# The third block's moved pairs: all tiles' scores in one half slice, a third buffer for transposed blocks, values around the second block's last second layer

## The chip, the cores and the metric

One Trainium2 chip, one of its cores. The time is device microseconds of one execution of the whole program; the kernel before took 667.09 us (median of three runs, 666.11 to 667.18).

## What is computed

Banded attention with a few global columns, then a two-layer network on its output, in float32. Batch 4, 8 heads, 768 positions, head size 64, so the network sees 3072 tokens of width 512 and has a hidden width of 2048.

```
scores = scale * q @ k^T                  # per batch and head, 768 x 768
keep   = (col < n_global) | (0 <= row - col < n_local)        # 8 and 96
scores = where(keep, scores - slope[head] * dist, -1e9)
a      = exp(scores - max) / (sum + 1e-9)
x      = (a @ v) as 3072 x 512
h      = x @ w_in                         # 512 x 2048
g      = h * clip(h + 3, 0, 6) / 6
out    = g @ w_out                        # 2048 x 512
```

## The kernel before

**Blocks, pairs, slices.** The 3072 tokens are cut into eight blocks of 384 (three tiles of 128). A block's attention is done by pairs of heads, four pairs to a block, numbered through: pairs 8 to 11 belong to the third block. Its network is done in 16 slices of the hidden width (f0 to f15). Every float32 product is done as three matmuls of a high and a low part (`w1h`, `w1l`, `xh`, `xl`, `gh`, `gl`).

**A slice** has two halves. First half: `first` (L161), 12 matmuls into a bank `hp`; then `gate` (ScalarE L178, VectorE L179) and the high part `gh` (GpSimd L185); the low part `gl` (VectorE L192) follows. Second half: `finish`, which runs `second` (L195), 9 matmuls, for the slice **before** it. So TensorE's order is first f9, second f8, first f10, second f9 and so on, and the `gh` and `gl` of a slice have the time of a second half and a first half to get ready. `halves` (L448) is a generator that stops after each half; between two stops the caller runs a list of closures, a *unit*, which holds attention work of a later block.

**A pair** in these units has these steps:

- `split(0..2)` (L810): ScalarE writes `q1` and GpSimd the high part of `kx` (step 0), VectorE writes `q2` (step 1, L828) and the low part of `kx` (step 2, L831), and step 2 then issues the load of the keys and queries of the pair two ahead. The buffers hold one pair, so step 0 has to come after the last score matmul of the pair before.
- `scores(t)` (L836) for t = 0, 1, 2: four matmuls into a bank, VectorE adds the distances and takes the least (L865), ScalarE the exponentials (L869).
- `sum_up`, `normalize(t)`: reciprocals on VectorE, then six GpSimd multiplications (L889).
- `spread(t)` (L904): VectorE turns 32 x 32 squares (L914) into a buffer `blocks`, and SyncE's queue writes it to DRAM (`there`); the first tile of pairs 8 to 11 has one transpose, the others two.
- `fetch` (L919): four transfers bring it back as `weights` with the squares in place.
- `values` (L932): twenty or twenty-four matmuls with `v` (L941), then ScalarE and VectorE write `xh`, `xl` of the block (`put_x`, L150), then the `v` of the pair two ahead is loaded.

**The stage of the change** ("one") runs from the last first-block slice to the start of the third block's network. In it the second block's slices f8 to f15 run, 16 half slices, and beside them the attention of pairs 9 to 11 (pair 8 was done earlier) and the splits of pair 12. The second block's sums occupy the banks `sp`, `tp` and `xp`, so scores and values share the three banks `acc`, in rotation. `rest_of_third` (L631) builds the units; `banded` (L589 to L600) makes the pools and runs them.

**What sets the order.** `in_order` (L621) ties TensorE, SyncE and GpSimd to the order in which the code is written. The order on VectorE and ScalarE is chosen by the scheduler when the program is built. All transfers of this stage are issued by SyncE, one after the other, and one that waits holds up those behind it.

After this stage the network of blocks three to eight runs in the same way, with the attention of the next block in the units of `attention` (L661), which the change doesn't touch except by the number of `blocks` buffers.

Of the kernel before, what the change touches and what calls it, by code (L numbers as in the profile page):

```python
# [20 lines left out]
NT = 3  # L21
# [4 lines left out]
NF = DF // P  # L26
# [16 lines left out]
EARLY = 9  # L43
# [7 lines left out]
ORDER = "101001010010010100100"  # L51
# [8 lines left out]
class Kernel:  # L60
# [433 lines left out]
    def banded(self, flag):  # L494
# [12 lines left out]
        with ExitStack() as early, ExitStack() as words:  # L507
            x0 = self.x_tiles(self.pool("x0", 1, ctx=early, side="right"))
            xs = [x0, self.x_tiles(), self.x_tiles()]
# [8 lines left out]
            with ExitStack() as ctx:  # L518
# [7 lines left out]
                pairs = [Pair(self, n, xs[n // NPAIR], True) for n in range(EARLY)]  # L526
# [55 lines left out]
            next_f, todo = [FIRST, 0], []  # L582
# [4 lines left out]
                pass  # L587
            self.decoded_to(2 * NF - 1)
        self.attending(self.ctx, 2, 3, 2, side="right")  # L589
        self.bp = self.pool("bp", 2, side="right")  # L590
        self.there = self.pool("there", 2, bass.MemoryType.DRAM)
        self.op = self.pool("op", 3, side="right")
        self.stage = "one"
        units, ahead = self.rest_of_third(xs[2])
        for k, _ in enumerate(self.halves([(1, f, xs[1], acc1) for f in range(next_f[1], NF)], True)):
            for unit in units[k]:
                unit()
        self.finish()
        for unit in units[k + 1]:
            unit()  # L600
        self.stage = "layers"
        x = xs[2]
        for i in range(2, len(self.blocks)):
            units, x_next = [], None
            if i + 1 < len(self.blocks):
                x_next = self.x_tiles()
                units, ahead = self.attention(i + 1, x_next, ahead)
            else:
                units = [[]] * 4 + [[lambda: self.doubt(flag)]]
# [7 lines left out]
            x = x_next  # L617
# [10 lines left out]
                        mybir.DependencyClass.NoSync, mybir.DependencyReason.DATA), reason="in_order")  # L628
                last[i.engine] = i.name

    def rest_of_third(self, x):  # L631

        units = [[] for _ in range(2 * NF)]
        pairs = [Pair(self, n, x, False) for n in range(EARLY, 3 * NPAIR + 1)]
        for k in range(3):
            pairs[0].split(k, False)
        units[1] += [lambda: self.load_next(EARLY, False)]
        for p, (me, after) in enumerate(zip(pairs, pairs[1:])):
            at = units[4 * p + 1:]
            for t, k in enumerate((0, 0, 1)):  # L640
                at[k].append(lambda t=t, me=me: me.scores(t)())
            last = after is pairs[-1]
            if not last:
                at[1].append(lambda after=after: after.split(0))
            k = 1 if last else 2
            at[k] += [me.sum_up] + [lambda t=t, me=me: me.normalize(t) for t in range(NT)]
            if not last:
                at[2].append(lambda after=after: after.split(1))
            at[k + 1] += [lambda t=t, me=me: me.spread(t) for t in range(NT)]
            if not last:  # L650
                at[3].append(lambda after=after: after.split(2))
            at[k + 1] += [me.fetch]
            if last:
                for k in range(3):
                    at[3 + k].append(lambda k=k, after=after: after.split(k))
                units[2 * (NF - ORDER.count("1"))] += [lambda a=pairs[p - 1]: a.values("x"), lambda me=me: me.values("s")]
        if EARLY % 2:
            units[9].append(lambda: pairs[0].values("x"))
        return units, pairs[-1]

    def attention(self, i, x, first):  # L661

# [358 lines left out]
```

## Time and profile before

| | |
|---|---|
| time, median of three runs | 667.09 us |
| the profiled execution's own time | 666.31 us |
| its span (first to last instruction) | 664.5 us |
| TensorE idle by its list of waits, in stage "one" | 2.8 us on transfers, 1.1 us on GpSimd |
| TensorE idle by its list of waits, 207 us to the end | none listed |
| granted TensorE clock | 0.999 |

A line of the timeline has the start in us from the span's start, the duration, the engine, the code line, the operation, what it writes and reads, and how many instructions the line stands for; a bracket at its end gives the idle time of the engine before it and what ended that. PE is TensorE, DVE VectorE, ACT ScalarE, POOL GpSimd, SPq the transfers that SyncE issues. Matmuls are pipelined, so their durations overlap; time lost on TensorE is read from one start to the next.

### The profile page before, as it was taken

What the parts mean: (1) busy time and instruction counts of PE and PEld (TensorE: products, weight loads), DVE (VectorE), ACT (ScalarE), POOL (GpSimd) and SP (SyncE); (2) the same over time, 40 slices, a digit from 0 to 9 for tenths busy, and PEclk for the clock granted to TensorE, in tenths of its full rate; (3) what the DMA queues carried; (4) which work ended last, traced back from release to release, by engine and by line L of the source; (5) the groups of instructions that cost most, each with busy time, mean ns of one, the idle gap of its engine ahead of it and who ended that gap; (6) DMA issues with size and microseconds to landing.
All of it is one profiled execution on the core that took longest, in us unless ns stands there. A gap on an engine that the chain in (4) does not pass through costs nothing.

```text
span 664.5 us, 11420 instructions
## 1 busy us (share of the span) xinstructions
PE 649.1 (98%) x3933; PEld 581.2 (87%) x3933; DVE 430.1 (65%) x1147; ACT 288.5 (43%) x752; POOL 202.8 (31%) x377
## 2 busy tenths in 40 slices
PE   9989999999998999999999999999999999999997
PEld 7768899988878999899999989999998999989995
DVE  6888999997855776376653877457662776432222
ACT  6896877775433333244314333143331444121111
POOL 5662000002531543043340544225340444302110
PEclk9999999999999999999999999999999999999999
DMA  8676444432574566525663366524654255510001
GB/s 295 172 234 207 143 146 156 149 105 88 142 189 144 136 157 184 159 87 144 164 169 103 96 173 183 158 72 130 159 154 129 79 152 142 143 49 1 1 1 53
DMA packets 67316, 88.86 MB, mean 134 GB/s; under 512 B 10288, under 2 KB 52016, under 8 KB 67248
## 3 DMA queue, kind: packets, MB, share of 16 engines
q1 hardware_dynamic: 66960, 87.77, 46.2%
q8 instruction: 33, 0.54, 0.3%
q14 instruction: 35, 0.29, 0.1%
q10 hardware_dynamic: 288, 0.26, 0.1%
HBM read 65.08 MB, written 22.94 MB: 132 GB/s over the span
## 4 chain that ended last, share of the span: by engine, by line
PE 80%; DVE 10%; DMA 3%; ACT 2%; issue 2%; POOL 1%; SPq 0%; POOLq 0%; DVEq 0%; ACTq 0%
PE hp L167 35%; PE acc L199 33%; PE xp L941 3%; PE sp L854 2%; PE tp L941 2%; PE tp L854 2%; DMA there<-blocks 1%; DVE wz L422 1%; DVE wz L418 1%; DMA weights<-there 1%; ACT n L869 1%; DVE gl L192 1%; DVE g L179 1%; DVE wz L410 1%; POOL n L889 1%
## 5 line engine op out<-in xcount | busy, mean ns | idle before, releaser
L178 ACT ACTIVATE g<-hp,small 128x384 f32<-128x384 f32 x127 | 73.6, 579 | 248.4 <-PE hp L167 223.5
L167 PE MATMUL hp<-xh,w1h 128*128 128x384 f32 x512 | 174.2, 340 | 0.4 <-ACT w1h L426 0.4
L167 PE MATMUL hp<-xh,w1l 128*128 128x384 f32 x512 | 173.0, 338 | 0.5 <-DVE w1l L415 0.5
L167 PE MATMUL hp<-xl,w1h 128*128 128x384 f32 x512 | 172.1, 336 | 0.0
L185 POOL TENSOR_SCALAR gh<-g 128x384 fp32r<-128x384 f32 x104 | 56.2, 540 | 313.6 <-DVE g L179 287.1
L199 PE MATMUL acc<-w2h,gl 128*128 128x512 f32 x336 | 133.3, 397 | 0.2 <-DVE gl L192 0.2
L199 PE MATMUL acc<-w2l,gh 128*128 128x512 f32 x336 | 132.5, 394 | 0.0
L199 PE MATMUL acc<-w2h,gh 128*128 128x512 f32 x336 | 132.0, 393 | 0.0
L179 DVE SCALAR_TENSOR_TENSOR g<-g,hp 128x384 f32<-128x384 f32 x128 | 69.8, 545 | 69.6 <-ACT g L178 69.1
L869 ACT ACTIVATE n<-n,least 128x232 f32<-128x232 f32 (+1 forms) x192 | 89.1, 465 | 51.5 <-DVE least L865 50.1
L192 DVE TENSOR_TENSOR gl<-g,gh 128x384 fp32r<-128x384 f32 x128 | 79.7, 622 | 46.8 <-POOL gh L185 46.8
L889 POOL TENSOR_SCALAR n<-n,sums 128x232 f32<-128x232 f32 (+1 forms) x186 | 98.4, 545 | 35.7 <-DVE sums L880 24.4
L167 PEld LDWEIGHTS hp<-xh,w1h 128*128 128x128 f32 x512 | 96.4, 188 | 6.6 <-issue 1.9
L167 PEld LDWEIGHTS hp<-xl,w1h 128*128 128x128 f32 x512 | 96.2, 188 | 3.7
L167 PEld LDWEIGHTS hp<-xh,w1l 128*128 128x128 f32 x512 | 96.0, 188 | 1.0 <-DVE w1l L415 0.8
L199 PEld LDWEIGHTS acc<-w2h,gl 128*128 128x128 f32 x336 | 63.0, 188 | 15.3 <-DVE gl L192 2.0
L199 PEld LDWEIGHTS acc<-w2h,gh 128*128 128x128 f32 x336 | 63.3, 188 | 10.3 <-POOL gh L185 0.3
L199 PEld LDWEIGHTS acc<-w2l,gh 128*128 128x128 f32 x336 | 63.2, 188 | 10.3
L914 DVE STREAM_TRANSPOSE blocks<-n 128x256 f32<-128x256 f32 x127 | 49.4, 424 | 31.7 <-POOL n L889 19.4
L825 POOL TENSOR_SCALAR kx<-load 64x504 fp32r<-64x504 f32 (+1 forms) x46 | 36.2, 788 | 97.8 <-PE hp L167 96.0
L865 DVE CUSTOM_DVE_ANT_0 n<-sp,d 128x232 f32<-128x232 f32 (+1 forms) x70 | 23.7, 375 | 32.2 <-PE sp L854 31.7
L869 ACT ACTIVATION_READ_ACCUMULATOR n<-n,least 128x1 f32 x192 | 36.0, 188 | 0.0
(118 smaller groups left out, 745.3 us busy)
## 6 DMA issues: line engine op xcount, KB each, us to landing
wst<-w SPq DMA_DIRECT2D x32, 512.0 KB, 3.5
there<-blocks SPq DMA_DIRECT2D x58, 256.0 KB, 2.6
load<-pairs SPq DMA_DIRECT2D x23, 636.0 KB, 5.2
load<-pairs SPq DMA_DIRECT2D x32, 384.0 KB, 4.4
weights<-there SPq DMA_DIRECT2D x48, 192.0 KB, 3.7
weights<-there SPq DMA_DIRECT2D x44, 160.0 KB, 3.4
out<-o SPq DMA_DIRECT2D x23, 256.0 KB, 2.2
load<-pairs SPq DMA_DIRECT2D x8, 444.0 KB, 4.1
```

The source lines that it names most:

```text
L167: self.nc.tensor.matmul(hp, lhsT=self.w1(w, f)[:, kt, :], rhs=a[:, kt, :], start=(n == 0), stop=(n == 3 * NKT - 1))
L178: nc.scalar.activation(out=g, in_=hp, func=AF.Relu, bias=self.three, scale=1.0)
L179: nc.vector.scalar_tensor_tensor(out=g, in0=g, scalar=6.0, in1=hp, op0=ALU.min, op1=ALU.mult)
L185: self.nc.gpsimd.tensor_scalar(out=gh, in0=g, scalar1=1.0, scalar2=0.0, op0=ALU.mult, op1=ALU.add)
L192: self.nc.vector.tensor_tensor(out=gl, in0=g, in1=gh.bitcast(F32), op=ALU.subtract)
L199: self.nc.tensor.matmul(acc[tt], lhsT=a[:, tk], rhs=self.w2(w, f), start=(f == 0 and j == 0), stop=(f == NF - 1 and j == 2))
L825: nc.gpsimd.tensor_scalar(out=part["kx"][own, c], in0=k[own, c], scalar1=1.0, scalar2=0.0, op0=ALU.mult, op1=ALU.add)
L854: nc.tensor.matmul(sp[j][:, lo:W], lhsT=q[:, t], rhs=part["kx"][:, c], start=(m == 0), stop=(m == 1))
L869: nc.scalar.activation(out=e[:, j, lo:W], in_=e[:, j, lo:W], func=AF.Exp, bias=self.least[:, i:i + 1], scale=-1.0, accum_out=self.sums[:, ...
L889: nc.gpsimd.tensor_scalar(out=e[:, j, lo:W], in0=e[:, j, lo:W], scalar1=over, scalar2=0.0, op0=ALU.mult, op1=ALU.add)
L914: nc.vector.transpose(out=blocks[:, :, s].rearrange("p b j q -> p j b q"), in_=e[:, :, c:c + P].rearrange("p j (b q) -> p j b q", b=4))
L941: nc.tensor.matmul(xps[j * D:(j + 1) * D, t * P:(t + 1) * P], lhsT=vt[0:K, t, j * D:(j + 1) * D], rhs=self.part(t, j, c, K), start=(c == 0 ...
```

## The change

Per pair, the three score tiles move from two half slices (0, 0 and 1) into one, normalisation moves from the third half slice to the second and the transposes and the fetch from the fourth to the third; pair 11 had its normalisation and transposes there already. The splits of pairs 10 and 11 each move one half slice ahead. `blocks` gets three buffers in place of two, for the rest of the program. The values of pair 9 move from behind the second layer of f11 to behind the first layer of f13, one half slice on; those of pair 10 from behind the second layer of f15 to ahead of it; those of pair 11 stay behind it. The arithmetic is the same.

```diff
-        self.bp = self.pool("bp", 2, side="right")
+        self.bp = self.pool("bp", 3, side="right")
...
-        units, ahead = self.rest_of_third(xs[2])
+        units, pairs = self.rest_of_third(xs[2], NF - next_f[1])
         for k, _ in enumerate(self.halves([(1, f, xs[1], acc1) for f in range(next_f[1], NF)], True)):
             for unit in units[k]:
                 unit()
         self.finish()
-        for unit in units[k + 1]:
-            unit()
+        pairs[-2].values("s")
         self.stage = "layers"
-        x = xs[2]
+        x, ahead = xs[2], pairs[-1]
...
-    def rest_of_third(self, x):
+    def rest_of_third(self, x, slices):
...
         for p, (me, after) in enumerate(zip(pairs, pairs[1:])):
             at = units[4 * p + 1:]
-            for t, k in enumerate((0, 0, 1)):
-                at[k].append(lambda t=t, me=me: me.scores(t)())
             last = after is pairs[-1]
-            if not last:
-                at[1].append(lambda after=after: after.split(0))
-            k = 1 if last else 2
-            at[k] += [me.sum_up] + [lambda t=t, me=me: me.normalize(t) for t in range(NT)]
-            if not last:
-                at[2].append(lambda after=after: after.split(1))
-            at[k + 1] += [lambda t=t, me=me: me.spread(t) for t in range(NT)]
-            if not last:
-                at[3].append(lambda after=after: after.split(2))
-            at[k + 1] += [me.fetch]
-            if last:
-                for k in range(3):
-                    at[3 + k].append(lambda k=k, after=after: after.split(k))
-                units[2 * (NF - ORDER.count("1"))] += [lambda a=pairs[p - 1]: a.values("x"), lambda me=me: me.values("s")]
-        if EARLY % 2:
-            units[9].append(lambda: pairs[0].values("x"))
-        return units, pairs[-1]
+            at[0] += [lambda t=t, me=me: me.scores(t)() for t in range(NT)]
+            at[1] += [me.sum_up] + [lambda t=t, me=me: me.normalize(t) for t in range(NT)]
+            at[2] += [lambda t=t, me=me: me.spread(t) for t in range(NT)] + [me.fetch]
+            for k in range(3):
+                at[k + 3 if last else k].append(lambda k=k, after=after: after.split(k))
+        units[10].append(lambda: pairs[0].values("x"))
+        units[2 * slices - 1].append(lambda: pairs[-3].values("x"))
+        return units, pairs
```

The file gets twelve lines shorter, so line numbers behind the change are lower by twelve (L854 is then L842, L941 L929, L914 L902).

**TensorE at the end of the stage.** Before: the last matmul of the second layer of f14, the whole of that of f15 (it reads `gh_2427`), then the values of pair 10 (`weights_2240`) and pair 11 (`weights_2353`).

```order
L199 MATMUL xp_1029<-w2h1_1025,gl_2398 128x512
L199 MATMUL sp_1027<-w2h1_1025,gh_2427 128x512
L199 MATMUL sp_1027<-w2l1_1026,gh_2427 128x512
L199 MATMUL sp_1027<-w2h1_1025,gl_2432 128x512
L199 MATMUL tp_1028<-w2h1_1025,gh_2427 128x512
L199 MATMUL tp_1028<-w2l1_1026,gh_2427 128x512
L199 MATMUL tp_1028<-w2h1_1025,gl_2432 128x512
L199 MATMUL xp_1029<-w2h1_1025,gh_2427 128x512
L199 MATMUL xp_1029<-w2l1_1026,gh_2427 128x512
L199 MATMUL xp_1029<-w2h1_1025,gl_2432 128x512
L941 MATMUL acc_2461<-weights_2240,load1_73 64x128 x10
L941 MATMUL acc_2475<-weights_2353,load0_72 64x128 x10
```

Of the change, the same place (pair 10's weights are now `weights_2222`):

```order
L199 MATMUL xp_1029<-w2h1_1025,gl_2398 128x512
L929 MATMUL acc_2443<-weights_2222,load1_73 64x128 x10
L199 MATMUL sp_1027<-w2h1_1025,gh_2427 128x512
L199 MATMUL sp_1027<-w2l1_1026,gh_2427 128x512
L199 MATMUL sp_1027<-w2h1_1025,gl_2432 128x512
L199 MATMUL tp_1028<-w2h1_1025,gh_2427 128x512
L199 MATMUL tp_1028<-w2l1_1026,gh_2427 128x512
L199 MATMUL tp_1028<-w2h1_1025,gl_2432 128x512
L199 MATMUL xp_1029<-w2h1_1025,gh_2427 128x512
L199 MATMUL xp_1029<-w2l1_1026,gh_2427 128x512
L199 MATMUL xp_1029<-w2h1_1025,gl_2432 128x512
L929 MATMUL acc_2475<-weights_2353,load0_72 64x128 x10
```

Pair 10's values now stand between the last two second layers, and those nine matmuls between the values of pair 10 and of pair 11.

**ScalarE around pair 11's exponentials.** Before: the exponentials of its first tile (128 wide), the copy `xh` of pair 9, those of its second tile, a gate, the two `q1` of pair 12, those of its third tile, a gate.

```order
L869 ACTIVATE n_2273,sums_2271<-n_2273,least_80 128x128 x2
L153 CAST xh_151<-acc_2292 128x384
L869 ACTIVATE n_2283,sums_2271<-n_2283,least_80 128x232 x2
L178 ACTIVATE g_2319<-hp_2306,small_70 128x384
L824 ACTIVATE q1_2388<-load1_73 128x384
L824 ACTIVATE q1_2393<-load1_73 128x384
L869 ACTIVATE n_2325,sums_2271<-n_2325,least_80 128x232 x2
L178 ACTIVATE g_2383<-hp_2370,small_70 128x384
```

Of the change, the same stretch:

```order
L812 ACTIVATE q1_2388<-load1_73 128x384
L812 ACTIVATE q1_2393<-load1_73 128x384
L857 ACTIVATE n_2273,sums_2271<-n_2273,least_80 128x128 x2
L857 ACTIVATE n_2283,sums_2271<-n_2283,least_80 128x232 x2
L857 ACTIVATE n_2293,sums_2271<-n_2293,least_80 128x232 x2
L178 ACTIVATE g_2315<-hp_2302,small_70 128x384
L153 CAST xh_151<-acc_2328 128x384
L178 ACTIVATE g_2383<-hp_2370,small_70 128x384
```

The `q1` of pair 12, which read its load (`load1_73`), now stand ahead of all six exponentials of pair 11, and the gate of slice f13 behind them.

**SyncE's queue in the middle of the stage.** Before: pair 9's three writes to `there`, the load of pair 12 (`load1_73`, 1272 columns), pair 9's four fetches into `weights_2111`; then the same for pair 10 with the load of pair 13; then the `v` of pair 11 (768 columns).

```order
L916 DMA there_2112<-blocks_2113 512x1x64
L916 DMA there_2112<-blocks_2116 512x1x128
L916 DMA there_2112<-blocks_2120 512x1x128
L292 DMA load1_73<-pairs 128x1272
L923 DMA weights_2111<-there_2112 32x4x320 x4
L916 DMA there_2241<-blocks_2242 512x1x64
L916 DMA there_2241<-blocks_2245 512x1x128
L916 DMA there_2241<-blocks_2249 512x1x128
L292 DMA load0_72<-pairs 128x1272
L923 DMA weights_2240<-there_2241 32x4x320 x4
L292 DMA load0_72<-pairs 128x768
```

Of the change:

```order
L904 DMA there_2094<-blocks_2095 512x1x64
L904 DMA there_2094<-blocks_2098 512x1x128
L904 DMA there_2094<-blocks_2102 512x1x128
L911 DMA weights_2093<-there_2094 32x4x320 x4
L292 DMA load1_73<-pairs 128x1272
L904 DMA there_2223<-blocks_2224 512x1x64
L904 DMA there_2223<-blocks_2227 512x1x128
L904 DMA there_2223<-blocks_2231 512x1x128
L911 DMA weights_2222<-there_2223 32x4x320 x4
L292 DMA load0_72<-pairs 128x1272
L292 DMA load0_72<-pairs 128x768
```

Each fetch now stands ahead of the load that used to go before it, so the loads of pairs 12 and 13 are issued behind fetches that wait for the writes ahead of them.

## The prediction

> **What bounds the kernel now.** I read the page's head first, then the list of TensorE's waits, then the busy time by stage, then the timeline.
>
> ```profile
> span 664.5 us, 11420 instructions
> PE 649.1 (98%) x3933; PEld 581.2 (87%) x3933; DVE 430.1 (65%) x1147; ACT 288.5 (43%) x752; POOL 202.8 (31%) x377
> ```
>
> ```profile
> PE acc L941 <- DMA weights<-there: 2.8, 2, 1.7
> PE sp L199 <- POOL gh L185: 1.1, 1, 1.1
> ```
>
> ```profile
> 156.00:207.00 51.00, 47.16 (x293) 41.90 (x292) 33.10 (x96) 22.01 (x64) 16.83 (x33) 1.00 0.64 181
> 207.00:236.60 29.60, 29.60 (x162) 27.07 (x162) 22.89 (x64) 11.78 (x38) 12.93 (x23) 1.00 0.36 97
> 354.00:650.00 296.00, 296.00 (x1738) 268.63 (x1737) 161.23 (x421) 93.25 (x253) 93.44 (x166) 1.00 0.39 106
> ```
>
> TensorE sets the time. After 207 us it is busy without a gap (29.60 of 29.60 us, 296.00 of 296.00), so nothing is to be won there, only lost. In stage "one" 51.00 − 47.16 = 3.84 us are idle, and the two lines of the wait list that belong to it make 3.9 us. That stage is what the change rewrites. The timeline of TensorE there:
>
> ```profile
> 159.00 1.05 PE L854 MATMUL acc<-kx,q 128*128 128x128 f32 x8
> 159.88 0.34 PE L167 MATMUL hp<-xh,w1h 128*128 128x384 f32 x1
> ...
> 178.40 1.05 PE L854 MATMUL acc<-kx,q 128*128 128x128 f32 x8
> 180.52 1.32 PE L941 MATMUL acc<-weights,load 128*64 128x128 f32 x20 [1.07 <-DMA weights<-there]
> 181.77 0.44 PE L167 MATMUL hp<-xh,w1h 128*128 128x384 f32 x1
> ...
> 192.78 0.39 PE L199 MATMUL sp<-w2h,gh 128*128 128x512 f32 x1
> ...
> 194.63 0.40 PE L199 MATMUL xp<-w2h,gl 128*128 128x512 f32 x1
> 196.12 0.50 PE L199 MATMUL sp<-w2h,gh 128*128 128x512 f32 x1 [1.09 <-POOL gh L185]
> ...
> 198.52 1.32 PE L941 MATMUL acc<-weights,load 128*64 128x128 f32 x20
> 201.52 1.32 PE L941 MATMUL acc<-weights,load 128*64 128x128 f32 x20 [1.68 <-DMA weights<-there]
> 202.77 0.44 PE L167 MATMUL hp<-xh,w1h 128*128 128x384 f32 x1
> ...
> 204.96 0.60 PE L854 MATMUL sp<-kx,q 128*128 128x232 f32 x4
> 205.40 0.34 PE L167 MATMUL hp<-xh,w1h 128*128 128x384 f32 x1
> ```
>
> The reader should measure from start to start, since ends overlap. Eight score matmuls take 159.88 − 159.00 = 0.88, four take 205.40 − 204.96 = 0.44, one pair's values 181.77 − 180.52 = 1.25. What three waits cost:
>
> - Pair 9's values start at 180.52 where 178.40 + 0.88 = 179.28 was possible: **1.24**.
> - The second layer of f15 starts at 196.12. The step inside a second layer is (194.63 − 192.78) / 8 = 0.23, so 194.86 was possible: 1.26. It then takes 198.52 − 196.12 = 2.40 where nine steps are 2.08: 0.32 more. Together **1.58**.
> - Pair 11's values start at 201.52 where 198.52 + 1.25 = 199.77 was possible: **1.75**.
>
> In all **4.57 us**, an upper bound of what this change can win.
>
> **The change, part by part.** No matmul is added or removed; up to 178.40 TensorE does the same work in another order (the third score tile ahead of a first layer, not behind it).
>
> *Pair 9's values* go one half slice and a score tile later, and their fetch is issued earlier. They start behind the first layer of f13: 178.40 + 1.32 (three score tiles) + 2.1 = 181.8. In the profile before they could run at 180.52 with a fetch in the old place. The 1.24 go.
>
> *Pair 10's values* are ready long before (their chain starts ten us before pair 11's) and now stand ahead of the second layer of f15, so `gh` of f15 has 1.25 us more. That alone is a hair short of 1.26, but VectorE's side is eased too:
>
> ```profile
> 192.59 0.77 DVE L914 STREAM_TRANSPOSE blocks<-n 128x256 f32<-128x256 f32 x2 [0.67 <-DMA there<-blocks]
> 193.39 1.39 DVE L831 TENSOR_TENSOR kx<-load,kx 64x504 fp32r<-64x504 f32 x2
> 194.81 0.56 DVE L179 SCALAR_TENSOR_TENSOR g<-g,hp 128x384 f32<-128x384 f32 x1
> ```
>
> The gate of f15 stood behind pair 11's last transposes, which waited 0.67 for a `blocks` buffer. With a third one that wait is gone. The 1.58 go.
>
> *Pair 11's values* decide. When does TensorE come to them? The stretch from 181.77 to 194.86 (first f13 to second f14, without a wait) is 13.09 long with one score tile in it. Now: 178.40 + 1.32 + (13.09 − 0.44) + 1.25 (pair 9) = 193.6, + 1.25 (pair 10) + 2.08 (second f15) = **197.0**, where it was 201.52. When is `weights` there? Step by step, with rows of before:
>
> ```profile
> 162.72 0.93 ACT L824 ACTIVATE q<-load 128x384 fp32r<-128x384 f32 x2
> 163.55 0.48 ACT L869 ACTIVATE n<-n,least 128x232 f32<-128x232 f32 x1
> ...
> 180.83 0.40 ACT L869 ACTIVATE n<-n,least 128x128 f32<-128x128 f32 x1 [3.72 <-DVE least L865]
> ```
>
> ```profile
> 187.99 2.46 POOL L889 TENSOR_SCALAR n<-n,sums 128x128 f32<-128x128 f32 x6 [1.35 <-DVE sums L880]
> 190.42 0.51 POOL L185 TENSOR_SCALAR gh<-g 128x384 fp32r<-128x384 f32 x1
> ```
>
> Pair 11's scores end at 178.40 + 1.32 + 0.2 = 179.9. ScalarE then writes the two `q1` of pair 12 first (their buffer is free only now), 0.93, to 180.9; then six exponentials, 2 x 0.40 and 4 x 0.47, to 183.6; then the gate of f13, 0.5, to 184.1. VectorE's gate 0.55, to 184.7; GpSimd's `gh` of f13 0.51, to 185.2 (the sums are done meanwhile); six normalisations 2.46, to 187.7; the last two transposes 0.77, to **188.5**. Before, those ended at 192.59 + 0.77 = 193.36 and the values started at 201.52, 8.16 later: write, four fetches, landing. So 188.5 + 8.16 = **196.7**, 0.3 ahead of TensorE. That is no cover to speak of: a wait of 0 to 0.8 is what I put there, 0.3 as the value.
>
> *New costs.* (a) Pair 9's third score tile now writes the third `acc` bank at 159.88, which ScalarE is still emptying:
>
> ```profile
> 157.81 1.99 ACT L56 ACTIVATE o<-acc 128x512 f32<-128x512 f32 x3
> ```
>
> It ends at 159.80, so between nothing and 0.1. (b) VectorE, ScalarE and GpSimd get a pair's work in a lump, and the gates of f9 and f11 stand behind it on VectorE and ScalarE. For f11: pair 10's scores end near 170.2, `q1` 171.1, six exponentials 173.8, gate 174.3; VectorE does six reductions, two `q2` and two `kx`, which by these rows
>
> ```profile
> 163.73 1.33 DVE L828 SCALAR_TENSOR_TENSOR q<-load,q 128x384 fp32r<-128x384 f32 x2
> ...
> 164.98 0.87 DVE L192 TENSOR_TENSOR gl<-g,gh 128x384 fp32r<-128x384 f32 x1
> ...
> 166.30 0.57 DVE L831 TENSOR_TENSOR kx<-load,kx 64x400 fp32r<-64x400 f32 x1
> ```
>
> end at 174.0, the sums by 174.4, the gate at 174.9, `gh` at 175.5, `gl` at 176.1 to 176.4. The second layer of f11 wants `gh` at 176.31 and `gl` two matmuls later, 176.77. Cover 0.4 to 0.8 us: nothing lost, at worst 0.3. (c) Behind this stage the scheduler puts `gl` behind the third pair of transposes for pairs 12 to 15. The tightest place:
>
> ```profile
> 264.42 0.56 DVE L192 TENSOR_TENSOR gl<-g,gh 128x384 fp32r<-128x384 f32 x1 [0.33 <-POOL gh L185]
> ```
>
> ```profile
> 266.13 0.40 PE L199 MATMUL acc<-w2h,gl 128*128 128x512 f32 x1
> ```
>
> It is done at 264.98 and used at 266.13: 1.15 of cover against at most 0.77 more. Nothing lost.
>
> One rule of the Trainium skill speaks against (b): SBUF — State Buffer, section "Who interferes with whom", says that a VectorE instruction with two SBUF inputs and a GpSimd instruction that reads SBUF exclude each other for a whole instruction. The row of 0.87 above ran beside GpSimd's `kx`, where another `gl` has 0.56, so the trace shows a price of 0.3, not a full block. By the rule, GpSimd's two `kx` would be added whole to VectorE's lump, which would put `gh` of f11 about 1.6 later and cost about 0.8 us; the sum below would be −3.4 in place of −4.2.
>
> **Sum.** −4.57 + 0.3 (pair 11) + 0.1 (a and b) = **−4.2 us**. The profiled execution took 666.31 us (span 664.5 and 1.8 around it), which gives 662.1. The median of before is 0.8 above that execution and two of three runs lie at 667.1, so I put half the distance on it: **662.5**.
>
> **Rivals.** About 0.2%, 1.3 us, is what a measurement of this kernel can tell from no change.
>
> 1. *The wait stays at pair 11's values, over 1 us.* The two numbers that meet there, 197.0 and 196.7, are each sums of ten rows. And `q1` of pair 12 may be late: its load is issued behind pair 9's fetch. SyncE's queue before, and the landing times of the seven loads of this stage:
>
> ```profile
> 172.54 0.57 SPq L292 DMA_DIRECT2D load<-pairs  x1
> 174.68 1.76 SPq L923 DMA_DIRECT2D weights<-there  x4
> ```
>
> ```profile
> DMA to landing us min/median/max: 4.5/5.4/7.9
> ```
>
> Pair 9's last write goes out 2.5 earlier than before, so the fetch runs from 172.2 to 173.9 and the load lands at 173.9 + 5.4 = 179.3, or 181.8 with the longest landing; ScalarE wants it at 180.0. At worst 1.9 are added to pair 11's chain. Left of the gain: 2 to 3.5 us, 663.2 to 664.8. For it: the thin cover. Against: two ways of adding up give the same end.
>
> 2. *The lump becomes the bound* (no change): the second layers of f9, f11 and f13 each wait over 1 us for `gh`. It takes 2 to 3 us more in the lump than the rows give (the cover of `gh` is 0.8 at f11 and more at the others); three such stalls of 1.2 take 3.6 of the 4.2 back: 666.1. Against: every term in (b) is from the longer of the rows.
>
> 3. *Slower:* the same load as in rival 1, but so late that it holds ScalarE. Behind `q1` on that engine stand six exponentials and the gate of f13, and behind that GpSimd's normalisation and the second layer of f13. Each us that the load lands after 180.0 moves pair 11's values by one. It eats the whole gain from a landing at 184.2 and makes the kernel measurably slower from 185.5, which is 11.6 after its issue, where the longest of seven took 7.9. At a landing of 186 the time is 668.3.
>
> 4. *The change doesn't move what it says:* the order of before and after shows that the scores, values and fetches stand where the code puts them, so this is left only as rival 1, where the wait is renamed.
>
> **Chances.** Forecast (gain 3.5 to 4.6 us) 0.66; rival 1, 0.21; rival 2, 0.07; rival 3, 0.06. Faster by over 0.2% is the first two, 0.87; within 0.2% 0.07; slower 0.06. The range starts at 666.11 − 4.6, about 661.4, and reaches to the end of rival 1, 664.8; what is left out is rivals 2 and 3 and a little of both ends.
>
> **What would show it.** Right: the wait list names no `gh` and no `there` row in stage "one", or only pair 11's values with under 0.8; pair 9's values start behind the first layer of f13 at about 181.8; the block's network starts at about 198.3 where it was 202.77; the two `q1` of pair 12 start near 180.0; from there on every TensorE row is the old one moved by 4 to 4.5 us. Wrong: a bracket of over 1 us at pair 11's values (rival 1), brackets `<-POOL gh` at f9, f11 or f13 (rival 2), `q1` waiting on its load (rivals 1 and 3), or a gap on TensorE after the start of the third block's network, which would be the reordered transposes.

## The result, and the profile after

| | before | after |
|---|---|---|
| time, median (lowest to highest of six runs) | 667.13 us (666.11 to 668.55) | **662.27 us** (661.89 to 663.39) |
| the profiled execution's own time | 666.31 us | 662.71 us |
| its span | 664.5 us | 660.9 us |
| granted TensorE clock | 0.999 | 0.998 |
| stage "one" in the profile | 43.77 us | 39.66 us |

The ratio is 0.9928, with a 95% interval of 0.9915 to 0.9941: **faster by 0.7%**. "Stage" is here, and below, the stretch from the start of pair 9's first score matmul to the start of the third block's network (159.00 to 202.77 before).

The list of TensorE's waits after, whole:

```profile
PE xp L929 <- DVE xl L154: 2.4, 5, 1.1
PE xp L929 <- issue: 1.4, 1, 1.4
PE xp L362 <- DVE small L104: 0.9, 1, 0.9
PE hp L167 <- DVE w1l L415: 0.5, 1, 0.5
PE hp L167 <- ACT w1h L426: 0.4, 1, 0.4
PE tp L885 <- ACT pt L889: 0.3, 1, 0.3
PE acc L199 <- DVE gl L192: 0.2, 1, 0.2
```

The two rows that the prediction read before (2.8 us on `weights<-there`, 1.1 us on `gh`) are gone; what is left lies before 156 us, ahead of the stage. The busy time by stage, with the same three stretches moved by the time won:

```profile
156.00:203.50 47.50, 47.50 (x296) 42.49 (x295) 31.91 (x96) 21.59 (x64) 16.40 (x33) 1.00 0.67 196
203.50:233.10 29.60, 29.60 (x162) 27.02 (x161) 22.73 (x66) 11.77 (x36) 12.64 (x23) 1.00 0.39 104
350.00:646.00 296.00, 296.00 (x1738) 268.74 (x1737) 160.92 (x421) 93.34 (x253) 93.50 (x166) 1.00 0.39 107
```

TensorE is now busy for 47.50 of 47.50 us in the stage, and the two later stretches are as full as before. Its timeline:

```profile
159.32 1.56 PE L842 MATMUL acc<-kx,q 128*128 128x128 f32 x12
160.72 0.34 PE L167 MATMUL hp<-xh,w1h 128*128 128x384 f32 x1
...
176.71 0.39 PE L199 MATMUL sp<-w2h,gh 128*128 128x512 f32 x1
...
178.79 1.50 PE L842 MATMUL acc<-kx,q 128*128 128x128 f32 x12
180.13 0.34 PE L167 MATMUL hp<-xh,w1h 128*128 128x384 f32 x1
...
182.34 1.32 PE L929 MATMUL acc<-weights,load 128*64 128x128 f32 x20
183.59 0.50 PE L199 MATMUL sp<-w2h,gh 128*128 128x512 f32 x1
183.92 0.39 PE L199 MATMUL sp<-w2l,gh 128*128 128x512 f32 x1
184.15 0.40 PE L199 MATMUL sp<-w2h,gl 128*128 128x512 f32 x1
...
194.23 1.32 PE L929 MATMUL acc<-weights,load 128*64 128x128 f32 x20
...
197.73 1.32 PE L929 MATMUL acc<-weights,load 128*64 128x128 f32 x20
198.98 0.44 PE L167 MATMUL hp<-xh,w1h 128*128 128x384 f32 x1
```

The stage starts at 159.32, 0.32 later than before, so 0.32 is taken off a time of after to set it beside one of before. The three values blocks carry no bracket, and neither does any second layer. The stage takes 198.98 − 159.32 = 39.66, which is 4.11 less than before.

### The profile page after: what moved, and what is told of

It is laid out like the page before. It is cut to its first block, busy times and chain, and to the rows that moved or that the text cites. A ratio compares the mean times of both kernels' runs of the same rounds, so it can differ in the third digit from the quotient of the medians.

```text
span 660.9 us, 11414 instructions
## 1 busy us (share of the span) xinstructions
PE 649.6 (98%) x3933; PEld 581.9 (88%) x3933; DVE 427.6 (65%) x1147; ACT 288.1 (44%) x752; POOL 202.2 (31%) x377
## 4 chain that ended last, share of the span: by engine, by line
PE 86%; DVE 9%; ACT 2%; issue 2%; POOL 0%; POOLq 0%; DVEq 0%; ACTq 0%
PE hp L167 37%; PE acc L199 33%; PE xp L929 3%; PE sp L842 2%; PE tp L929 2%; PE tp L842 2%; PE sp L199 1%; ACT n L857 1%; DVE wz L422 1%; PE tp L199 1%; DVE wz L418 1%; PE xp L199 1%; DVE wz L410 1%; DVE g L179 1%; DVE gl L192 1%
## 5 line engine op out<-in xcount | busy, mean ns | idle before, releaser
L902 DVE STREAM_TRANSPOSE blocks<-n 128x256 f32<-128x256 f32 x127 | 48.8, 422 | 27.0 <-POOL n L877 26.8
```

The costliest lines, as they stand in the source:

```text
L902: nc.vector.transpose(out=blocks[:, :, s].rearrange("p b j q -> p j b q"), in_=e[:, :, c:c + P].rearrange("p j (b q) -> p j b q", b=4))
```

## The experiments

Twelve runs of eleven kernels were made, in three groups, each beside runs of the kernel before on the same chip. None leaves out a part of the computation. The stage's time is from one profiled execution, the median from all runs; "waits" are TensorE's in the stage.

| kernel | `blocks` | scores and normalisation | values 9 / 10 | median (lowest to highest, runs) | ratio, 95% interval | stage | waits of TensorE listed |
|---|---|---|---|---|---|---|---|
| before (two profiles) | 2 | old | old / old | 667.1, 666.1 and 667.1 in the three groups | | 43.77, 43.62 | 1.07, 1.09, 1.68; 1.02, 0.77, 1.86 |
| e1_buffer | 3 | old | old / old | 663.67 (663.08 to 664.83, 9) | 0.9946, 0.9931 to 0.9961 | 41.43 | 0.37, 1.10 |
| e2_ahead | 2 | old | old / new | 667.54 (665.82 to 669.38, 10) | 1.0005, 0.9987 to 1.0022 | 44.84 | 0.78, 3.03 |
| e3_lump | 2 | new | old / old | 668.58 (665.76 to 669.37, 10) | 1.0014, 0.9995 to 1.0033 | 44.95 | 2.61, 0.74 |
| e4_two | 2 | new | new / new | 667.21 (665.85 to 668.90, 10) | 1.0004, 0.9987 to 1.0022 | 44.37 | 0.34, 2.00, 0.37 |
| e7_both_old, e7_again | 3 | new | old / old | 663.11 (662.62 to 663.87, 4), 662.92 (662.31 to 665.09, 10) | 0.9951, 0.9934 to 0.9967; 0.9938, 0.9924 to 0.9952 | 41.20, 41.63 | 0.27, 0.82; 0.26, 1.30 |
| e9_moves_buffer | 3 | old | new / new | 663.84 (662.84 to 664.51, 5) | 0.9961, 0.9946 to 0.9975 | 41.18 | 0.25, 0.85 |
| e10_late_load | 2 | new, one load later | new / new | 665.36 (664.16 to 667.00, 10) | 0.9982, 0.9969 to 0.9996 | 41.54 | 1.78 |
| e5_nine_old | 3 | new | old / new | 662.40 (662.29 to 663.92, 5) | 0.9935, 0.9912 to 0.9958 | 39.78 | none |
| e6_ten_old | 3 | new | new / old | 662.50 (661.79 to 664.42, 6) | 0.9935, 0.9912 to 0.9957 | 40.32 | 0.49 |
| after, after_again | 3 | new | new / new | 662.27, 662.61 (662.11 to 662.84, 5) | 0.9928; 0.9934, 0.9912 to 0.9956 | 39.66, 39.66 | none |

**Theory A** was the prediction's: each of the three waits is set by its own chain, and the parts of the change take away the shares that the prediction gave them. The rivals were B (the places of the values decide), C (putting all three tiles' scores, then the normalisation, in one half slice each, the "lump", does it all), and for the writes to `there`, D (a write is slow because transfers issued just ahead fill the queues) against E (a write behind a full `blocks` costs that by itself).

**e1_buffer: before, with the third buffer alone.**

```diff
-        self.bp = self.pool("bp", 2, side="right")
+        self.bp = self.pool("bp", 3, side="right")
```

> The kernel before with the third blocks buffer alone. Measure: start of pair 9's first score to start of the third block's network, 43.77 us before, 39.66 us after the change. Theory A (each wait is set by its own chain): the last transposes of pairs 9 and 11 go ahead of gl and no longer wait for a write, about 1 us earlier each. Pair 9's wait (1.07) nearly goes, f15's (1.09) falls to about 0.3, pair 11's stays at 1.2 to 2.0 since its chain and TensorE both come earlier: stage 41.9, time 1.9 us less. Theory B (the places of the values decide, the buffer matters little): stage 43.3 to 43.8, time 0 to 0.5 less.

The waits of TensorE in 156 to 206 us of e1:

```profile
PE acc L941 <- DMA weights<-there: 1.1, 1, 1.1
PE sp L199 <- POOL gh L185: 0.4, 1, 0.4
```

One number does 2.3 of the 4.1 us that the stage lost in the profile (43.77 to 41.43), and 667.1 to 663.67 in the medians. A was right in direction but had put the stage at 41.9; B (43.3 or more) failed. Pair 9's wait is gone with no matmul moved. Where it came from is seen in SyncE's queue; the three writes of pair 9, of pair 10 and of pair 11, before:

```profile
168.79 3.64 SPq L916 DMA_DIRECT2D there<-blocks  x3
...
179.37 3.57 SPq L916 DMA_DIRECT2D there<-blocks  x3
...
189.22 4.68 SPq L916 DMA_DIRECT2D there<-blocks  x3
```

and in e1, with pair 9's fetch, which before was issued at 174.68:

```profile
168.59 2.58 SPq L916 DMA_DIRECT2D there<-blocks  x3
...
173.51 1.76 SPq L923 DMA_DIRECT2D weights<-there  x4
179.00 2.58 SPq L916 DMA_DIRECT2D there<-blocks  x3
...
188.37 2.58 SPq L916 DMA_DIRECT2D there<-blocks  x3
```

With two buffers the third write waits for the first to land, 1.0 to 2.1 us in every pair, and the fetch with it: before, the first writes landed at 171.10, 181.61 and 192.57, and the last transposes of the three pairs started at 171.12, 181.63 and 192.59. VectorE's timeline before has a bracket at only one of the three places (0.67, at pair 11): at the other two VectorE reduced the first of pair 10's and 11's scores and wrote a `gl` meanwhile, so that no wait for `there` was listed although the last transposes were late.

**e2_ahead: before, with pair 10's values ahead of the second layer of f15.**

```diff
-                units[2 * (NF - ORDER.count("1"))] += [lambda a=pairs[p - 1]: a.values("x"), lambda me=me: me.values("s")]
+                units[15].append(lambda a=pairs[p - 1]: a.values("x"))
+                units[16].append(lambda me=me: me.values("s"))
```

> The kernel before with pair 10's values alone put ahead of the second layer of f15. Theory A: the wait at f15 goes, but pair 11's weights come no earlier, so its wait grows from 1.68 to about 3.2: stage 43.7 (0.3 either way), time unchanged. Theory B: the 1.58 at f15 are won, stage 42.2, time 1.6 less.

The wait of f15 went, as expected, and the wait at pair 11's values grew by as much, as expected. B (42.2) failed. What A had not foreseen (it had 43.7) is the row's duration and the stretch around it (the columns of the second view are the stretch, then busy time and count of TensorE, of its weight load, VectorE, ScalarE and GpSimd, then the granted clock, the transfers' share and GB/s):

```profile
201.82 2.40 PE L942 MATMUL acc<-weights,load 128*64 128x128 f32 x20 [3.03 <-DMA weights<-there]
204.15 0.69 PE L167 MATMUL hp<-xh,w1h 128*128 128x384 f32 x1
```

```profile
202.00:204.00 2.00, 2.00 (x20) 1.82 (x19) 0.00 (x0) 0.00 (x0) 0.00 (x0) 0.50 0.99 321
```

After 3.03 us of waiting the clock was granted at half, and the values took 204.15 − 201.82 = 2.33 where 1.25 is usual. That is why the stage came out at 44.84, above before. A moved wait saved nothing.

**e4_two: the change with two buffers.**

```diff
-        self.bp = self.pool("bp", 3, side="right")
+        self.bp = self.pool("bp", 2, side="right")
```

> The change with two blocks buffers. Theory A: pair 11's last transposes wait 1.5 to 2 us for a write, its values then wait 1 to 2 us: stage 41.2 (0.7 either way), time 2.5 less than before, 1.6 more than the change. Theories B and C: the buffer matters little, stage 39.7 to 40.0.

A's number failed by 3 us, that of B and C by over 4: without the third buffer the whole rest of the change wins nothing. VectorE and TensorE in e4:

```profile
193.39 0.77 DVE L902 STREAM_TRANSPOSE blocks<-n 128x256 f32<-128x256 f32 x2 [3.56 <-DMA there<-blocks]
194.09 0.52 DVE L192 TENSOR_TENSOR gl<-g,gh 128x384 fp32r<-128x384 f32 x1
```

```profile
194.66 0.50 PE L199 MATMUL sp<-w2h,gl 128*128 128x512 f32 x1 [2.00 <-DVE gl L192]
...
196.65 2.40 PE L929 MATMUL acc<-weights,load 128*64 128x128 f32 x20
```

VectorE stood 3.56 us before pair 11's last transposes, because the first write had not landed, and the `gl` of f14 was queued behind them. TensorE waited 2.00 for that `gl`, and then the clock fell here too (values at 2.33 again, 196.65 to 198.98).

**e10_late_load: e4 with the load of pair 13 issued behind pair 11's fetch**, to tell D from E. The second argument of `split` says whether its step 2 issues the load.

```diff
-                at[k + 3 if last else k].append(lambda k=k, after=after: after.split(k))
+                at[k + 3 if last else k].append(lambda k=k, p=p, after=after: after.split(k, p != 1))
+        units[12].append(lambda: self.load_next(EARLY + 2, False))
```

> The change with two buffers, and with the load of pair 13 (636 KB) issued behind pair 11's fetch, not ahead of its writes. With two buffers and the load ahead, the write of pair 11's first tile took 5.0 us to land and VectorE waited 3.56 for it; stage 44.4. Theory D (the write is slow because the transfers just ahead of it fill the 16 engines): it lands in 3 to 3.5, VectorE waits 1.5 to 2, TensorE's 2.0 at the second layer of f14 falls below 0.6, stage 42.3 to 43. Theory E (a write after two buffers costs that much by itself): no change, stage 44 to 44.6.

The times from issue to landing of pair 11's three writes to `there`, of e4 (the two longer ones are those of the first two writes):

```profile
DMA to landing us min/median/max: 2.5/4.6/5.0
```

and of e10, with the row of VectorE's last transposes:

```profile
DMA to landing us min/median/max: 2.5/2.5/2.6
```

```profile
191.73 0.77 DVE L903 STREAM_TRANSPOSE blocks<-n 128x256 f32<-128x256 f32 x2 [1.01 <-DMA there<-blocks]
```

D holds: with one load less just ahead, the first two writes landed in 2.5 us where e4's took 5.0 and 4.6, VectorE's wait fell from 3.56 to 1.01, the wait for `gl` of f14 went, and 2.8 us of the stage came back (44.37 to 41.54, the fall of the clock in e4 included). D had asked for less, a stage of 42.3 to 43. The medians show less too: e4 is 0.1 above the kernel before beside it, e10 is 0.8 below. The 1.78 that is left stands at pair 11's values; the list names nothing that ended it, but the last of the fetches landed at 200.19 and the values started at 200.42. So the change carries a price of its own, the loads close ahead of pair 11's write, and the third buffer is what keeps it from reaching VectorE.

**e3_lump: the change with two buffers and the values in their old places.**

```diff
-        self.bp = self.pool("bp", 3, side="right")
+        self.bp = self.pool("bp", 2, side="right")
...
+        for unit in units[k + 1]:
+            unit()
...
-        units[10].append(lambda: pairs[0].values("x"))
-        units[2 * slices - 1].append(lambda: pairs[-3].values("x"))
+        units[9].append(lambda: pairs[0].values("x"))
+        units[2 * slices].append(lambda: pairs[-3].values("x"))
```

> The change without the third buffer and with the values of pairs 9 and 10 in their old places: the lump alone. Theory A: pair 9's wait goes (its fetch is 2.5 us earlier), but with two buffers pair 11's last transposes wait 1.5 to 2 us for a write, so f15 waits over 1 us for gh and pair 11's values over 1 us: stage 42.3 (0.7 either way), time 1.5 less. Theory C (the lump does it all): stage 39.7 to 40.0, time 4 less. Theory B: stage 43 or more.

A and C both missed. B's number (43 or more) fits, but not its reason: e4, with the values in the new places, is as slow. The wait moved to pair 9's values, which share the three `acc` banks with pair 11's scores. VectorE and TensorE in e3:

```profile
181.33 0.77 DVE L904 STREAM_TRANSPOSE blocks<-n 128x256 f32<-128x256 f32 x2 [1.36 <-DMA there<-blocks]
182.02 0.25 DVE L855 CUSTOM_DVE_ANT_0 n<-acc,d 128x128 f32<-128x128 f32 x1
```

```profile
182.55 2.32 PE L931 MATMUL acc<-weights,load 128*64 128x128 f32 x20 [2.61 <-DVE least L855]
```

VectorE stood before pair 10's last transposes and read the scores of pair 11 out of the banks only from 182.02 on. TensorE could not write a bank until then, and the clock fell once more. e3 and e4 show the same thing at two places: in the new order VectorE has so much work behind the transposes that a full `blocks` stops TensorE.

**e9_moves_buffer: before, with the third buffer and both moves of values, without the lump.** The edit is that of e1 and e2 and

```diff
-            units[9].append(lambda: pairs[0].values("x"))
+            units[10].append(lambda: pairs[0].values("x"))
```

> The kernel before with the third buffer and both moves of the values, scores in two half slices as before (no lump). Pair 11's third score tile is issued 1.4 us earlier than with the buffer alone, since pair 9's values no longer stand ahead of it. Theory A: pair 11's weights land about 0.4 after TensorE comes to them: stage 40.0 (0.4 either way), time 0.3 to 0.5 more than the change. Theory C (the lump is needed for the last third of the gain): stage 41 to 41.4, as with the buffer alone.

The wait of 0.85 at pair 11's values says that without the lump its weights come too late. C's number (41 to 41.4) fits, A's does not. By the medians the two moves without the lump win nothing over the buffer alone (663.84 against 663.67, each beside its own runs of before).

**e7_both_old: the change with both moves undone** (lump and buffer), and e7_again, the same kernel once more. The edit is that of e3 without its first two lines.

> The change with the values of pairs 9 and 10 in their old places (lump and third buffer only). Theory A (each wait is set by its own chain; with three buffers pair 9's weights are there by 177.5 and gh of f15 by 194.1): nothing is lost, stage 39.5 to 39.9 us from pair 9's first score to the third block's network, time within 0.3 us of the change. Theory B (the moves of the values are needed): a wait of over 1 us at pair 9's values or at f15, stage 40.7 to 42.

> The change with the values of pairs 9 and 10 both in their old places, profiled a second time. In the first profile the stage took 41.20, with 0.27 listed at the second layer of f15 and 0.82 at pair 11's values, whose write was 3.5 us from its issue to the fetch where the change's took 2.7. If the longer write belongs to the order, the stage takes 41.0 to 41.4 again and the write is again over 3.2; if it was chance, the write takes 2.5 to 2.9 and the stage 40.2 to 40.6.

In both profiles about 1.5 to 2 us of the gain is missing, and in both the write of pair 11 lands late. A's 39.5 to 39.9 failed; B's 40.7 to 42 fits, but the wait is at pair 11's values, where B had not put it. In e7_again the write took 3.7 us to the fetch, over the 3.2 that was asked for, and the stage, 41.63, lies above the 41.0 to 41.4. The landing times of the transfers of `there` in 186 to 192 us, of e7_both_old:

```profile
DMA to landing us min/median/max: 3.9/4.0/4.5
```

and of after:

```profile
DMA to landing us min/median/max: 3.1/3.2/3.7
```

The second profiles have 4.1/4.3/4.7 (e7_again) and 3.5/3.6/4.1 (after_again).

The medians say less: 663.11 and 662.92, where the change has 662.27 and 662.61. The execution of e7_again that was profiled took 664.63, the second longest of its ten. So the 1.54 us of the first profile overstates what the two moves are worth on the mean; by the medians it is 0.3 to 0.8 us, and the ranges of the runs overlap.

**e5_nine_old and e6_ten_old: one move undone each.** Theory N gave the moves' worth to pair 9, theory M to pair 10. e5 and e6:

```diff
-        units[10].append(lambda: pairs[0].values("x"))
+        units[9].append(lambda: pairs[0].values("x"))
```

```diff
+        for unit in units[k + 1]:
+            unit()
...
-        units[2 * slices - 1].append(lambda: pairs[-3].values("x"))
+        units[2 * slices].append(lambda: pairs[-3].values("x"))
```

> The change with the values of pair 9 alone in their old place (behind the second layer of f11, so ahead of the first layer of f13); pair 10's values in the new place. It splits the 1.54 us that both moves together were worth in the stage (41.20 with both old, 39.66 with the change). Theory N (pair 9's move carries it): with the values ahead of the first layer of f13, the gate of f13, gh and then the normalisation and transposes of pair 11 come about 0.6 later on the stage's clock and the write collides longer with the loads, so the weights of pair 11 come about 1.5 later while TensorE comes to them no later: a wait of 1.2 to 1.5 at pair 11's values, stage 40.9 to 41.3. Theory M (pair 10's move carries it, because gh of f15 is late without it): no wait at f15, under 0.5 at pair 11, stage 39.7 to 40.2.

> The change with the values of pair 10 alone in their old place, behind the second layer of f15; pair 9's in the new place. Theory N (pair 9's move carries the 1.54): the second layer of f15 starts 0.3 to 0.5 late (gh), and this time is taken from the way to pair 11's values, whose weights are there by then: no wait at pair 11 or under 0.3, stage 40.0 to 40.3. Theory M (pair 10's move carries it): stage 40.9 to 41.3, with a wait of over 0.7 at pair 11's values.

N fails at e5 (39.78, no wait, where it asked for 40.9 to 41.3), M fails at e6 (40.32 with a wait of 0.49, where it asked for 40.9 to 41.3). Neither move carries the 1.54; either one alone keeps most of it, and both kernels run as fast as the change (662.40 and 662.50). Undoing pair 10's move has the larger price in the profile, 0.66 against 0.12. (The list puts the 0.49 of e6 down to a load, but the last of pair 11's fetches landed at 197.90 and the values started at 198.14.)

**before_again and after_again**: both kernels profiled a second time without an edit.

> The kernel before, profiled once more, to see how far its stage varies between executions. If its waits on transfers vary, the stage lies anywhere from 43.5 to 45 us; if not, it is 43.8 within 0.1.

> The changed kernel itself, profiled a second time, to see by how much the stage's time differs from one execution to the next without any edit. If the margin at pair 11's values is as thin as I worked out, a second profile can show a wait of up to 0.5 there and a stage of 39.66 to 40.2; if there is room, the stage is 39.6 to 39.75 and nothing is listed there.

Before's three waits fall differently from one execution to the next (1.07, 1.09, 1.68 and 1.02, 0.77, 1.86) though their sum is nearly the same. The change gave 39.66 twice.

## Why the prediction was right, step by step

**The bound and the 4.57.** Right. The three waits are gone, almost nothing was won or lost behind the stage (from the network's start to the end of the span 461.7 before, 461.9 after), and 4.11 of the 4.57 came off in the profile.

**Pair 9's values** (1.24). Started at 182.34, on before's clock 182.02; the forecast was 181.8. The wait is gone, but the reason given, a later place and an earlier fetch, is not the one that was needed: e1 loses this wait with the buffer alone, the values in their old place, because the last write leaves 1 us earlier.

**Second layer of f15** (1.58). Gone. e2 shows that pair 10's values ahead of it do that alone; e1 shows that the buffer alone leaves 0.37.

**Pair 11's values** (1.75 less 0.3). No wait, so the 0.3 that the sum put there was 0. The two ends that the forecast set against each other were TensorE's arrival at 197.0 and the weights at 196.7. TensorE came at 197.73 − 0.32 = 197.41. For the weights, the chain on ScalarE, GpSimd and VectorE after, in one row or two of each:

```profile
180.04 0.94 ACT L812 ACTIVATE q<-load 128x384 fp32r<-128x384 f32 x2 [2.55 <-PE acc L842]
```

```profile
184.85 0.51 POOL L185 TENSOR_SCALAR gh<-g 128x384 fp32r<-128x384 f32 x1 [5.89 <-DVE g L179]
185.34 2.86 POOL L877 TENSOR_SCALAR n<-n,sums 128x128 f32<-128x128 f32 x6
```

```profile
185.40 0.56 DVE L192 TENSOR_TENSOR gl<-g,gh 128x384 fp32r<-128x384 f32 x1 [0.24 <-POOL gh L185]
...
187.37 1.64 DVE L902 STREAM_TRANSPOSE blocks<-n 128x256 f32<-128x256 f32 x4 [0.43 <-POOL n L877]
```

`gh` ends at 185.36, on before's clock 185.04 (forecast 185.2), the transposes at 189.01, so 188.69 (forecast 188.5): the ten rows added up to within 0.2. One term was off, the six normalisations, 2.86 for 2.46. The 2.46 came from a pair that had no `gl` beside it; after, a `gl` of VectorE, with both inputs in SBUF, runs beside their start in all three pairs. Its own 0.56 is unchanged, but GpSimd's first normalisation is drawn out. All eighteen normalisations of the stage, in ns, least, median and longest:

```profile
L877 POOL TENSOR_SCALAR n<-n,sums x18: 367/455/772, 165.6 to 187.8; 128x232 f32<-128x232 f32 x12, 128x128 f32<-128x128 f32 x6
```

The 0.77 is the first of each six, a narrow one; the second, as narrow, takes 0.37. The Trainium skill, SBUF — State Buffer, section "Who interferes with whom", would have a whole instruction excluded; here GpSimd was the slower one, by 0.40, less than the 0.56 of the whole `gl`. The four fetches went out from 192.21 on; the last was issued at 193.54 and landed 3.82 us later, at 197.36, so 0.37 ahead of TensorE at 197.73, where the forecast had 0.3. The real room is less. Wherever TensorE did wait for this fetch, it started about 0.24 us after the last landing (before: landed at 201.28, started at 201.52), which leaves about 0.1 us here and, with a landing at 197.01 and a start at 197.32, as little in after_again. That nothing was listed at this place in either profile is a matter of a tenth of a microsecond.

**The lump** (b). The cover held. `gh` of f11 was ready at 175.64 and its second layer began at 176.71. The price of 0.8 by the skill's rule did not come: GpSimd's two `kx` ran from 170.44 to 171.56, and VectorE's first `q2` began at 171.64, so at this place the two did not meet, and the rule was not put to a test there. What the prediction did not see is that the lump also makes a full `blocks` dear (e3, e4); in the profile after, VectorE is not listed as waiting for a write in the stage or behind it.

**The bank** (a). The three score tiles of pair 9 took 160.72 − 159.32 = 1.40 where pair 11's took 1.34: 0.06, in its bounds.

**Behind the stage** (c). Busy 29.60 of 29.60 us. Nothing lost.

**What the sum left out.** Each change between values and a layer costs about 0.1. After pair 9's values the first step of a second layer took 183.92 − 183.59 = 0.33 where the next took 0.23. There are now three blocks of values among the layers, each with an entry and an exit, where pairs 10 and 11 stood next to each other before. Five of these changes lie between the scores of pair 11 and its values; at 0.1 each they are about the 0.4 by which TensorE comes to them later (197.41 on before's clock) than the forecast 197.0. The network starts at 198.66, 0.36 after the forecast 198.3.

**What was luck.** The 198.3 and the sum do not agree: the 198.3 leaves out the 0.3 that the sum puts at pair 11's values, and the sum's −4.2 would give 198.6. So the sum came out at the stage's 4.11 because two errors of about the same size cancelled, a wait of 0.3 that did not come and some 0.4 of changes between layers and values that were not counted. The forecast for the profiled execution, 662.1, was too low: it took 662.71, 3.60 less than before, since its stage began 0.32 later and 0.2 was lost behind it. The median met the forecast (662.27 for 662.5) although the prediction put it 0.4 above the profiled execution and it came out 0.4 below.

**The rivals.** `q1` of pair 12 waited for TensorE's scores, not for its load (the row at 180.04), so neither the late load of rival 1 nor rival 3 came, and no wait was left at pair 11's values; no second layer waited for `gh`, so rival 2 did not come; and the parts did what the code says.

**The weights given to the parts.** This is what the prediction had most wrong, though the sum does not show it. The third buffer got 0.67 us, at one wait of VectorE, because only that wait had a bracket. By e1 it wins 2.3 us of the stage alone, and by e4 the rest of the change wins nothing without it (44.37, where 39.66 is reached with it).

**The median.** It fell by 4.86, more than the stage's 4.11 and more than the 4.57 that the prediction called an upper bound, which counts the waits of one execution whose clock did not fall. Of 61 runs of before that came beside the experiments, 40 had a mean granted clock of 0.998 or more and a median of 666.25; 21 had less, and a median of 667.76. The changed kernel's eleven runs all had 0.998 or more, and of all 50 runs of kernels with the third buffer two had less. The difference between the first group and after is 3.98, the stage's gain. That before loses the rest to a clock that falls now and then at its longest wait is what the last section makes likely; no profile of before caught it.

## What to carry to other kernels

A wait for a buffer need not show as idle time: where the engine has other work to put in, look instead at when the instruction that needs the buffer starts, and at a group of DMA issues that is longer than their number explains (3.64 for 2.58). Before moving work around a wait, ask what else the moved work queues in front of: the same new order won 4.9 us in the median with one buffer more and nothing without it. A wait that is moved is not a wait won: in e2 it was taken away at one place and came back whole at the next.

## What the hardware showed that was not expected

Leaving aside the end of the program, where TensorE has nothing left to do and the clock falls too, in four of the fourteen profiles the granted clock fell to half, once and for about 3.4 us, around a gap of TensorE: of 2.00 us (e4), of 2.61 (e3), of 3.03 (e2), and of 1.85 in e10, far ahead of the stage. It stayed at 1.00 after gaps of 1.68 and 1.86 (before, twice), of 1.78 (e10, in the stage) and of 2.02 (e7_again, at the same early place). The two early gaps, e10's first:

```profile
44.21 2.68 PE L930 MATMUL xp<-pt,load 128*64 128x128 f32 x24 [1.85 <-issue]
```

```profile
44.03 1.54 PE L931 MATMUL xp<-pt,load 128*64 128x128 f32 x24 [2.02 <-issue]
```

The same matmuls took 2.68 us behind the shorter gap and 1.54 behind the longer one. So the length of a gap alone does not tell whether the clock falls; near 2 us it may or may not, and no run told what else decides. e4 by single microseconds, the gap being the one that ended at 194.66:

```profile
195.00:196.00 1.00, 1.00 (x6) 0.82 (x5) 0.97 (x2) 0.28 (x1) 0.00 (x0) 1.00 0.61 179
196.00:197.00 1.00, 1.00 (x7) 0.47 (x7) 0.57 (x2) 0.00 (x0) 0.21 (x1) 0.60 0.29 84
197.00:198.00 1.00, 1.00 (x14) 1.00 (x12) 0.56 (x1) 0.00 (x0) 0.30 (x1) 0.50 0.11 26
198.00:199.00 1.00, 1.00 (x11) 0.67 (x8) 0.00 (x0) 0.00 (x0) 0.00 (x0) 0.50 0.90 279
199.00:200.00 1.00, 1.00 (x5) 0.85 (x4) 0.40 (x1) 0.48 (x1) 0.00 (x0) 0.69 1.11 233
```

Here the fall came over a microsecond after the work had begun again; in e3 and e10 it came within 0.2 us of that, and in e2 just before. By the clock's column it cost 0.40 + 0.50 + 0.50 + 0.31 = 1.7 us beside the gap itself. The runs agree: of the ten of e3, the two with a mean clock of 0.999 or more took 665.76 and 665.92, the eight others, at 0.994 to 0.996, 667.29 to 669.37. The Trainium skill, TensorE: Matmul & The Clock Gate, section "Why this matters for your kernels", asks for no idle gaps over about 3 us; here falls came with gaps of 1.85 to 3.03.

Still open is why pair 11's writes land later with both values in their old places (medians 4.0 and 4.3 us in the two profiles of e7, 3.2 and 3.6 in those of after, 3.1 in e5 and e6), although the loads ahead of them are the same and stand as far ahead. Those two loads were slow themselves, 6.0 to 6.7 us from issue to landing in e7 and 4.8 to 6.1 in the others, so whatever it is acts before the writes. No run told the cause.
